# Expert routing in a fused attention and mixture kernel: positions, dummy products, and address tables per expert

## Chip, core and metric

The kernel runs on one core of a Trainium2 chip. The metric is device microseconds of one execution; a kernel's time is the median of its runs. An engine is named as the profile names it: PE is TensorE, DVE is VectorE, ACT is ScalarE, POOL is GpSimd, SP issues DMAs.

## What is computed

Attention in which each query keeps its 32 largest scores, then a soft mixture of experts (every token sends a weighted share to 32 slots), then a mixture in which each token goes to its two best experts of eight:

```python
def _moe2_ref(x, w_gate, w_noise, noise, w1, w2):      # x: 2304 x 512, w1: 8 x 512 x 1024, w2: 8 x 1024 x 512
    logits = x @ w_gate
    noisy_logits = logits + np.log1p(np.exp(x @ w_noise)) * noise
    top2 = np.argpartition(-noisy_logits, 2, axis=1)[:, :2]
    top2_l = np.take_along_axis(noisy_logits, top2, axis=1)
    top2_w = softmax(top2_l)                            # over the two
    for e in range(8):
        for k in range(2):
            mask = top2[:, k] == e
            h = np.maximum(x[mask] @ w1[e], 0.0)
            out[mask] += top2_w[mask, k, None] * (h @ w2[e])
    return out
```

x is itself a product of a 2304 x 32 matrix (the combine weights of the soft mixture, `cn`) with a 32 x 512 matrix of slot outputs (`so`). The kernel never forms x: it multiplies the slot outputs into the weights of each expert first ("expert e's weights" below are 32 x 1024), and routes rows of 32 numbers.

## The kernel before

The order of work is written out by hand: every engine executes its instructions in the order in which the program issues them, and semaphores make one engine wait for another. All products of float32 accuracy after the routing are made of three products of a high and a low half (`hh`, `hl`, `wh`, `wl`); the low half is a "correction" that VectorE subtracts.

The middle of the run has these stages, in `moe` and `gated`.

- *First mixture* (lines 825 to 906): eight experts' weights stream through; products per expert, the last expert's in two halves. Its end waits for the last weights.
- *Slot outputs and logits* (lines 907 to 1009): `cn` is transposed into `ct` (L912, L913), the slot outputs `sos` are folded (L823) into `soT`; the gate weights (L981) and `ct` (L989) give the logits of all tokens. Then expert 0's weights are multiplied (`weigh01`, L952, four quarters of eight products), while ScalarE and VectorE make the noisy logits `ng` and each token's eight largest (`m8`, L1009).
- *Routing of expert 0* (lines 1020 to 1170): one-hot `oh` (L1023), mask `mb` (L1026). TensorE first subtracts the high half of expert 0's weights (L1029, the correction), then counts, for each token, the tokens before it with the same expert (L1032 and 17 products of L1035): the position. `slot1` (L1042) holds expert 0's positions. `compact(t)` compares the positions of 128 tokens with the slot numbers (VectorE, L1148; four of 18 on ScalarE) and a product with the result (L1152) moves the tokens' rows to their slots. Expert 1's weights are multiplied between them.
- *Ramp* (`gated`, from line 1297): expert by expert, 64 chunks `n` = 8 e + c, with five products `acc` of three halves each per chunk. Chunk n issues `split(n + 2)` (halves of the second weights), `first(n + 2)` (L1254, then hh on ACT L1259 and hl on DVE L1260) and `second(n)` (L1278 to L1280). `first(n + 2)` needs the one buffer `hp`, which `hl` of the chunk before frees. After chunk 7 of an expert `store` scales the five accumulators (ACT and DVE in turn, L1288, L1290) and scatters them from GpSimd's queue (L1291); the next expert's `second` overwrites them.
- *Address tables* (`addresses`, `spread`, `rows_of_slots`): each token's slot number of 8 x 640 is split into a low part (slot modulo 128) and a column; one-hot tables of both, for 36 groups of 128 choices, are made by GpSimd, ScalarE and VectorE in chunk 0, and 36 products (L1125) in chunk 2 give the row number for every slot of all experts. Then GpSimd gathers rows by indirect DMA (`rows(e)`, L1223): expert 1 in chunk 2, expert 0 in chunk 4 (only its gates and token numbers are needed), expert 2 in chunk 6; `slots` and `turn` (L1242) bring them into place.

`order`, `slot` and `MORE` fix when the DMA queue of SP issues each expert's weights and into which buffer.

Of the kernel before, what the change touches and what calls it, by code (L numbers as in the profile page):

```python
# [8 lines left out]
F32 = mybir.dt.float32  # L9
F32R = mybir.dt.float32r  # L10
BF = mybir.dt.bfloat16
# [22 lines left out]
ED = 1  # L34
ONACT = (2, 6, 10, 14)
# [7 lines left out]
def moe_after_topk_attention(ctx: ExitStack, tc: tile.TileContext, q, k, v, phi, w1, w2, wg, wn, noise, u1, u2, qk, vt, qr, out):  # L43
# [3 lines left out]
    def pool(name, bufs=1, stack=ctx, **kw):  # L47
# [59 lines left out]
             + [(2, 0), (2, 1), (3, 0), (2, 2), (3, 1), (2, 3), (2, 4), (2, 5), (3, 2), (2, 6), (2, 7)]  # L107
# [3 lines left out]
    slot = [*range(11), 0, 1, 2, 3, 4] + [6, 0, 1, 2, 5, 6, 0, 2, 6, 1, 5] + [0, 2, 1, 5, 6]  # L111
# [64 lines left out]
    FW = (18, 19)  # L176

# [609 lines left out]
    def moe(st, xp, xs, fast):  # L787
# [26 lines left out]
        def warm(n):  # L814

            p = bank("acc0")
            for _ in range(n):
                T.matmul(p, onesb, onesb.unsqueeze(1).to_broadcast([128, 4, 128]), start=True, stop=True)
# [66 lines left out]

        sx, so = bank("acc2"), [bank(f"acc{n}") for n in range(2)]
        sos = ww[:, F + 2048:F + 2560]
        for e in range(E):
# [19 lines left out]
        ct = tb.tile([128, 5, 128], F32, name="ct")  # L908
        cf = cn.rearrange("p t s -> p (t s)")
        pc = [bank(x) for x in ("acc3", "acc2")]  # L910
        for g in range(4):
            T.transpose(pc[0][:, g * 128:g * 128 + 128], cf[:, g * 128:g * 128 + 128], identf)  # L912
        T.transpose(pc[1][:64, :128], cf[:, 512:576], identf)  # L913
        p = fold_t(sos, 4, fold)
        A.copy(ct[:, 0:4], pc[0].rearrange("p (a b) -> p a b", a=4))
        A.copy(ct[:64, 4], pc[1][:64, :128])
# [108 lines left out]
        mb = small("mb", BF)  # L1025
        V.tensor_tensor(mb, oh[:, 0], oh[:, 1], op=OP.add)  # L1026
        V.tensor_tensor(gw[:, 1], m8[:, :, 1], m8[:, :, 0], op=OP.subtract)
        for r, (x, h, _) in enumerate(quarters(0, P0)):
# [134 lines left out]
        for e in range(2):  # L1163
            used(2, e)
# [371 lines left out]
```

## Time and profile before

| | us |
|---|---|
| median of 3 runs | 753.01 (751.64 to 753.68) |
| profiled execution, its own time | 754.7 |
| its span, first to last instruction | 752.8 |

| engine | busy us | share of the span |
|---|---|---|
| PE matmul | 726.1 | 96% |
| PE weight load | 596.4 | 79% |
| DVE | 556.1 | 74% |
| POOL | 501.1 | 67% |
| ACT | 488.9 | 65% |

The shares are means over stages with different limits; matmuls are pipelined and overlap, so a busy PE isn't PE at its peak. The mean granted clock of TensorE over the span is 0.984 of full speed.

### The profile page before, as it was taken

The numbers are of one execution on the slowest core, as the hardware profiler recorded it, in microseconds if no ns is written. First come the engines' busy times: TensorE is split into PE (matmuls) and PEld (weight loads), VectorE is DVE, ScalarE is ACT, GpSimd is POOL, SyncE is SP. The second block draws the span as 40 slices with busy tenths as digits, with TensorE's granted clock in tenths as the row PEclk, the third lists the DMA queues.
The fourth block names the chain that finished last, engine by engine and source line by source line (L and its number), as shares of the span: only waits on it lengthen the run. The fifth ranks groups of instructions, "written<-read, shape, count | busy, mean of one in ns | idle before, by whom it ended". The sixth has DMA issues, their size and how long they took to land.

```text
span 752.8 us, 17317 instructions
## 1 busy us (share of the span) xinstructions
PE 726.1 (96%) x5670; PEld 596.4 (79%) x5670; DVE 556.1 (74%) x2632; ACT 488.9 (65%) x1025; POOL 501.1 (67%) x633
## 2 busy tenths in 40 slices
PE   9999999999999999999999998889999999999994
PEld 4789999898998889998898434567876888888883
DVE  7999999998999999999984404956554556555550
ACT  5999999999999999999995204742222222322320
POOL 4999999998999989999774030455551527344034
PEclk9999999999999999999999996999999999999998
DMA  6247687867786445544558799769774985344055
GB/s 222 51 114 224 184 227 211 224 193 185 205 223 187 108 119 112 130 112 110 155 217 284 267 392 344 263 255 346 177 144 139 320 279 72 61 65 61 1 64 72
DMA packets 62455, 133.99 MB, mean 178 GB/s; under 512 B 13330, under 2 KB 14354, under 8 KB 62354
## 3 DMA queue, kind: packets, MB, share of 16 engines
q1 hardware_dynamic: 55314, 122.59, 54.1%
q0 software_dynamic: 7040, 10.18, 9.8%
q8 instruction: 47, 0.77, 0.4%
q14 instruction: 54, 0.44, 0.2%
HBM read 85.02 MB, written 17.97 MB: 137 GB/s over the span
## 4 chain that ended last, share of the span: by engine, by line
PE 52%; DVE 26%; POOL 10%; issue 6%; DMA 3%; ACT 1%; SPq 0%; POOLq 0%; DVEq 0%; ACTq 0%
DVE c L506 10%; PE acc L1280 9%; PE acc L1279 9%; PE acc L1278 9%; DVE TH L537 5%; PE av L570 5%; POOL u L529 5%; DVE c L513 4%; PE S L468 3%; POOL s L544 2%; PE hp L1254 2%; PE st L549 2%; DVE mx L509 2%; DMA wx<-in_moe_w_dram 2%; PE acc L832 2%
## 5 line engine op out<-in xcount | busy, mean ns | idle before, releaser
L506 DVE MAX8 c<-s 128x8 f32<-128x82 f32 (+1 forms) x1008 | 221.4, 229 | 3.7 <-ACT s L486 3.0
L529 POOL TENSOR_TENSOR u<-g,s 128x576 f32<-128x576 bf16 x144 | 186.7, 1297 | 9.2 <-ACT g L523 9.2
L570 PEld LDWEIGHTS av<-vb,et 128*128 128x128 f32 (+1 forms) x1600 | 165.4, 180 | 11.2 <-issue 8.3
L570 PE MATMUL av<-vb,et 128*128 128x65 f32 (+1 forms) x1600 | 173.1, 263 | 0.8 <-ACT et L556 0.8
L1291 POOL DMA_INDIRECT out_dram<-y,ii x40 | 64.8, 1621 | 121.6 <-issue 60.2
L1259 ACT ACTIVATE hh<-hp 128x640 fp32r<-128x640 f32 x62 | 43.8, 707 | 136.9 <-PE hp L1254 136.9
L1278 PE MATMUL acc<-wh,hh 128*128 128x512 f32 x320 | 127.1, 397 | 0.6 <-DVE hl L1260 0.6
L1280 PE MATMUL acc<-wh,hl 128*128 128x512 f32 x320 | 126.9, 397 | 0.7 <-DVE hl L1260 0.7
L1279 PE MATMUL acc<-wl,hh 128*128 128x512 f32 x320 | 126.3, 395 | 0.0
L544 POOL TENSOR_SCALAR s<-s,mx 128x576 f32<-128x576 f32 x144 | 108.4, 753 | 21.2 <-ACT a L543 13.9
L537 DVE MAX8 TH<-u 128x8 f32<-128x584 f32 x144 | 109.1, 758 | 14.5 <-POOL u L530 13.6
L1260 DVE SCALAR_TENSOR_TENSOR hl<-hp,hh 128x640 fp32r<-128x640 f32 x62 | 51.1, 824 | 91.2 <-ACT hh L1259 91.1
L543 ACT ACTIVATE a<-s,TH 128x576 bf16<-128x576 f32 x144 | 117.4, 815 | 0.1
L549 PE MATMUL st<-identf,s 128*128 128x128 f32 x576 | 115.2, 281 | 1.4 <-POOL s L544 0.8
L523 ACT ACTIVATE g<-s,T 128x576 bf16<-128x576 f32 x144 | 116.4, 808 | 0.0
L550 PE MATMUL st<-steep,a 128*128 128x128 bf16 x576 | 105.5, 219 | 0.0
L468 PE MATMUL S<-ks,qs 128*128 128x288 f32 x560 | 105.1, 313 | 0.0
L488 ACT ACTIVATE s<-S 128x576 f32<-128x576 f32 x141 | 96.8, 687 | 4.5 <-PE S L477 2.6
L561 ACT ACTIVATE et<-st 128x512 f32<-128x512 f32 x144 | 90.4, 628 | 3.2 <-PE st L550 2.5
L549 PEld LDWEIGHTS st<-identf,s 128*128 128x128 f32 x576 | 83.6, 145 | 9.9 <-POOL s L544 3.3
L468 PEld LDWEIGHTS S<-ks,qs 128*128 128x128 f32 x560 | 78.6, 189 | 1.8
L1278 PEld LDWEIGHTS acc<-wh,hh 128*128 128x128 f32 x320 | 60.6, 190 | 14.9 <-issue 2.7
(339 smaller groups left out, 1151.0 us busy)
## 6 DMA issues: line engine op xcount, KB each, us to landing
wa<-in_moe_w_dram SPq DMA_DIRECT2D x8, 2048.0 KB, 13.9
wa<-in_moe_w_dram SPq DMA_DIRECT2D x28, 512.0 KB, 6.9
wb<-in_moe_w_dram SPq DMA_DIRECT2D x5, 2048.0 KB, 9.8
ks<-hl SPq DMA_DIRECT2D x56, 160.0 KB, 2.8
ks<-raw SPq DMA_DIRECT2D x56, 160.0 KB, 3.1
raw<-in_qk_dram SPq DMA_DIRECT2D x14, 608.0 KB, 4.5
wy<-in_moe_w_dram SPq DMA_DIRECT2D x4, 2048.0 KB, 9.3
wb<-in_moe_w_dram SPq DMA_DIRECT2D x16, 512.0 KB, 8.1
```

The source lines that it names most:

```text
L468: T.matmul(ph[hf][:, :288], QS[h][:, q0:q0 + 128], KS[h][:, l, ks], start=(n == 0), stop=(n == len(mm) - 1))
L506: V.max(C[i][:, c * 8:c * 8 + 8], SS[i][:, cut[c]:cut[c + 1]])
L523: A.activation(g, SS[i], AF.Sign, bias=last8(T24, i, 1), scale=-OVER, accum_out=SM[:, i:i + 1])
L529: G.tensor_tensor(u[:, 0:S], G1[i], SS[i], op=OP.mult)
L537: V.max(last8(TH, i), UU[i])
L543: A.activation(AP[i // 2][:, S * (i % 2):S * (i % 2) + S], SS[i], AF.Relu, bias=last8(TH, i, 1), scale=-1.0)
L544: G.tensor_scalar(SS[i], SS[i], -1.0, MX[i][:, 0:1], op0=OP.mult, op1=OP.add)
L549: T.matmul(o, SP[i // 2][:, ks], identf, start=True, stop=True, is_transpose=True)
L570: T.matmul(av[h][o:o + m, tt * 65:tt * 65 + 65], x, VB[j % 2][:, h, c if c < 4 else 4 + i % 2], start=(c == 0), stop=(c == 4), tile_positi ...
L1278: T.matmul(ACC[j], HH[n][:, r], WH[n], start=(c == 0), stop=False)
L1279: T.matmul(ACC[j], HH[n][:, r], WL[n], start=False, stop=False)
L1280: T.matmul(ACC[j], HL[n][:, r], WH[n], start=False, stop=(c == 7))
```

## The change

- The transposes of `cn` (`turn_c`) are issued ahead of the last expert of the first mixture. The fold of the slot outputs is written out, with two dummy products (`warm`, 512 columns of ones) between its halves and two behind it.
- The first quarter of expert 0's products stands ahead of the logits' product, the other three behind it, followed by nine dummy products.
- The mask comes straight from `ng` and `m8`, ahead of the one-hot; the positions come ahead of the correction of expert 0's weights.
- `slot1` holds the positions of experts 0 and 1 (`ED` 2). ScalarE makes three of the 18 compares (7, 11, 15). Expert 1's first two quarters of products come ahead of all compaction.
- The routed rows are written to DRAM from GpSimd's queue.
- The address tables are made in three parts. Expert 1 and expert 0 have their own (18 groups of 128 tokens each): columns by GpSimd (`slots_of`) beside the compaction, compares by VectorE, one per group (`hots_of`), 18 products each in chunks 2 and 4. Experts 2 to 7 share one: addresses in chunk 5, columns in chunk 6 (VectorE), compares in chunks 6 to 9 (VectorE and ScalarE), 36 products in chunk 9.
- The weights of expert 3 are loaded ahead of the second weights of expert 1. The flags for the rare cases are made in chunk 21, with a new test of ties (`keep_tie`). Expert 2's slots and turns come one chunk later.

```diff
-ED = 1
-ONACT = (2, 6, 10, 14)
+ED = 2
+ONACT = (7, 11, 15)
...
-             + [(2, 0), (2, 1), (3, 0), (2, 2), (3, 1), (2, 3), (2, 4), (2, 5), (3, 2), (2, 6), (2, 7)]
+             + [(2, 0), (2, 1), (3, 0), (2, 2), (2, 3), (3, 1), (2, 4), (2, 5), (3, 2), (2, 6), (2, 7)]
...
+    LATER = 21
...
+        def turn_c():
+            cf = cn.rearrange("p t s -> p (t s)")
+            x = halves()
+            for g in range(4):
+                T.transpose(x[:, 0, g * 128:g * 128 + 128], cf[:, g * 128:g * 128 + 128], identf)
+            T.transpose(x[:64, 1, :128], cf[:, 512:576], identf)
+            A.copy(ct[:, 0:4], x[:, 0].rearrange("p (a b) -> p a b", a=4))
+            A.copy(ct[:64, 4], x[:64, 1, :128])
...
             if e == E - 2:
                 A.copy(sos, sx)
+                turn_c()
...
+        p = bank()
+        for c in range(4):
+            if c == 2 and fast:
+                warm(2, "acc3")
+            T.matmul(p[:, c * 32:c * 32 + 32], sos[:, c * 128:c * 128 + 128], fold, start=True, stop=True)
+        p = p[:, :4 * NS].rearrange("p (c s) -> p c s", s=NS)
+        if fast:
+            warm(2, "acc3")
...
+        if fast:
+            P0, P1 = bank("acc1"), bank("tp")
+            weigh01(0, 0, P0)
         ggd = tb.tile([128, 4, 16], F32, name="ggd")
...
         if fast:
-            P0, P1 = bank("acc1"), bank("tp")
-            for c in range(4):
+            for c in range(1, 4):
                 weigh01(0, c, P0)
+            warm(9, "acc2")
...
+        mb = gp.tile([128, TT, 8], BF, name="mb")
+        V.tensor_tensor(mb, ng, m8[:, :, 1:2].to_broadcast([128, TT, 8]), op=OP.is_ge)
         V.tensor_tensor(oh, ng.unsqueeze(1).to_broadcast([128, 2, TT, 8]),
...
-            nc.sync.dma_start(XD[0:2 * NTOK].rearrange("(p r) f -> p (r f)", p=128), RW.rearrange("p c t f -> p (c t f)"))
+            G.dma_start(XD[0:2 * NTOK].rearrange("(p r) f -> p (r f)", p=128), RW.rearrange("p c t f -> p (c t f)"))
...
+        def hot(o, x, on_act=False):
+            if not on_act:
+                for i in range(x.shape[-1]):
+                    V.tensor_scalar(o[:, i], ntb, x[:, i:i + 1], None, op0=OP.is_equal)
+                return
...
+        def slots_of(e):
...
+            for j in range(JT + 1):
+                G.tensor_scalar(ge[:, :, j], slot1[:, :, e], 128.0 * j + 1, 0.0, op0=OP.is_ge, op1=OP.add)
+            G.tensor_tensor(eq, ge[:, :, 0:JT], ge[:, :, 1:], op=OP.subtract)
+            G.tensor_scalar(w, oh[:, 1, :, e], float(TT), 0.0, op0=OP.mult, op1=OP.add)
+            G.tensor_tensor(w, w, ctn[:, 0:TT], op=OP.add)
+            G.tensor_tensor(x[:, :, 0], eq, w.unsqueeze(2).to_broadcast([128, TT, JT]), op=OP.mult)
+            G.tensor_scalar(x[:, :, 1], eq, pn, 0.0, op0=OP.mult, op1=OP.add)
...
             def columns():
...
+                V.tensor_tensor(eq, nt[:, 2 * JT:E * JT].unsqueeze(1).to_broadcast([128, 2 * TT, m]),
+                                pc[:, 1].unsqueeze(2).to_broadcast([128, 2 * TT, m]), op=OP.is_equal)
+                V.tensor_tensor(x[:, :, 0], eq, ctn.unsqueeze(2).to_broadcast([128, 2 * TT, m]), op=OP.mult)
+                V.tensor_scalar(x[:, :, 1], eq, pn, None, op0=OP.mult)
...
-        more(20)
-        for n, c in zip((3, 3, 3, 3), range(4)):
+        used(2, 0)
+        more(21)
+        for e in (1, 0):
+            slots_of(e)
+        for n, c in zip((0, 0, 2, 3), range(4)):
             some(n)
             weigh01(1, c, P1)
-        for e in range(2):
-            used(2, e)
-        some(2)
+        used(2, 1)
+        some(7)
         gates()
+        low_of()
         some(TT)
...
             if n == 0:
-                begin()
-                for k in range(3):
-                    far(k)
-                    near(k)
-                columns()
-                partitions()
-                for k in range(3, 5):
-                    same(k)
+                halve1(1, P1)
+                hots_of(t2, 1, (0,))
+            if n == 1:
+                hots_of(t2, 1, (1, 2))
...
             if n == 3:
-                first_weights2(ps.tile([128, 512], F32, name="tp"))
+                first_weights2(tp())
+                hots_of(t2, 0, range(3))
             if n == 4:
+                p1 = tp()
+                join_of(0, p1)
+                rows_in(t2, p1, 0, 1)
+                rows(0)
+                ids_of(0)
                 slots(1)
-                rows(0)
             if n == 5:
                 turn(1, 0, 4)
+                addresses()
             if n == 6:
-                ids_of(0)
+                columns, hots, join = spread(t2)
+                columns()
+                hots(0, True)
+            if n == 7:
+                hots(2, False)
+            if n == 8:
+                hots(1, True)
+                for i in (3, 4):
+                    hots(i, False)
+            if n == 9:
+                hots(5, False)
+                p1 = tp()
+                join(p1)
+                rows_in(t2, p1, 2, E - 2)
                 rows(2)
-            if n == 9:
                 ids_of(2)
+            if n == LATER:
+                later(t2)
...
-                if c == 3 and e:
+                if c == (4 if e == 1 else 3) and e:
                     slots(e + 1)
-                if c == 4 and e:
+                if c == (5 if e == 1 else 4) and e:
                     turn(e + 1, 0, 4)
```

`hots`, `join`, `hots_of`, `join_of` and `store` stand in program order within a chunk as the list shows; `store` is issued last in chunk 7.

## Rows read from the trace of the kernel before

**Rows 1.** Stretches: PE, PEld, DVE, ACT, POOL busy (count), clock, DMA share, GB/s.
```profile
456.30:470.00 13.70, 11.44 (x87) 5.99 (x90) 7.07 (x35) 8.01 (x18) 0.00 (x0) 0.50 0.96 317
...
488.20:493.20 5.00, 1.63 (x37) 1.46 (x36) 4.97 (x5) 3.80 (x6) 2.96 (x2) 1.00 0.93 338
...
493.90:497.20 3.30, 3.30 (x9) 2.61 (x8) 1.99 (x6) 1.13 (x2) 1.93 (x2) 0.50 1.02 416
...
500.00:735.00 235.00, 234.06 (x1123) 186.44 (x1122) 129.03 (x221) 64.02 (x100) 97.00 (x80) 1.00 0.59 141
```

**Rows 2.** Chain of waits, 430 to 512 us: start, us, what.
```profile
433.82 17.46 DMA wx<-in_moe_w_dram
...
457.51 3.61 PE acc L952 x32
...
501.16 3.57 PE tp L1210 x32
```

**Rows 3.** Instructions in order of time, compaction: start, us, what, [idle before].
```profile
465.35 2.80 DVE L1148 TENSOR_SCALAR wx<-nt,slot 128x128 fp32r<-128x128 f32 x7
...
473.56 1.95 PE L1152 MATMUL acc<-wx,xw 128*64 128x320 f32 x12
```

**Rows 4.** Instructions in order of time, SP's queue: expert 0's weights issued.
```profile
439.12 2.54 SPq L134 DMA_DIRECT2D wb<-in_moe_w_dram  x1
```

**Rows 5.** DMA issues at that time: KB each, median us to landing.
```profile
wb<-in_moe_w_dram SPq DMA_DIRECT2D x1, 2048.0 KB, 17.1
```

**Rows 6.** Instructions in order of time, logits to positions.
```profile
455.61 1.90 PE L989 MATMUL acc<-ggd,ct 128*128 128x64 f32 x10 [0.45 <-DVE ggd L984]
...
457.55 0.29 ACT L1001 ACTIVATE na<-acc 128x144 f32<-128x144 f32 x1 [3.35 <-PE acc L989]
...
459.27 1.32 DVE L1009 MAX8 nz<-T 128x8 f32<-128x8 f32 x18
...
461.11 0.31 DVE L1026 TENSOR_TENSOR mb<-oh 128x144 bf16<-128x144 f32 x1
...
463.69 0.30 PE L1032 MATMUL acc<-mb,before 128*128 128x144 bf16 x1
```

**Rows 7.** Instructions in order of time, ramp: VectorE beside GpSimd.
```profile
478.57 6.51 POOL L1095 TENSOR_TENSOR y<-nt,pc 128x1024 bf16<-128x1024 f32 x3 [36.26 <-ACT hh L1259]
...
478.98 2.04 DVE L1270 TENSOR_TENSOR wl<-wa,wh 128x512 fp32r<-128x512 f32 x1
```

**Rows 8.** VectorE's groups by shape, 430 to 600 us: busy us, mean ns, idle before.
```profile
L1270 DVE TENSOR_TENSOR wl<-wb,wh 128x512 fp32r<-128x512 f32 x16 | 11.2, 698 | 0.5
...
L1109 DVE TENSOR_TENSOR eq<-nt,pc 128x800 bf16<-128x800 f32 x1 | 1.0, 984 | 0.0
...
L1148 DVE TENSOR_SCALAR wx<-nt,slot 128x128 fp32r<-128x128 f32 x1 | 0.3, 286 | 0.1
```

**Rows 9.** Instructions in order of time, GpSimd, 430 to 480 us.
```profile
437.15 0.66 POOL L850 COPY RW<-LT 128x576 f32<-128x576 f32 x1
437.75 0.21 POOL L851 COPY RW<-ids 128x18 f32<-128x18 f32 x1
```

**Rows 10.** Instructions in order of time, ramp: chunks, turns, corrections.
```profile
477.24 0.51 PE L1278 MATMUL acc<-wh,hh 128*128 128x512 f32 x1
...
506.03 1.39 DVE L1216 TENSOR_TENSOR gl<-tp,gh 64x512 fp32r<-64x512 f32 x2 [5.32 <-ACT gh L1213]
...
513.53 0.33 PE L1242 MATMUL tp<-identf,cx 128*128 128x128 f32 x1 [0.68 <-ACT cts L1244]
...
515.08 0.46 PE L1254 MATMUL hp<-cts,gs 128*128 128x320 f32 x2
...
516.31 0.82 DVE L1260 SCALAR_TENSOR_TENSOR hl<-hp,hh 128x640 fp32r<-128x640 f32 x1 [3.31 <-ACT hh L1259]
...
526.82 0.46 PE L1254 MATMUL hp<-cts,gs 128*128 128x320 f32 x2
...
530.56 0.46 PE L1254 MATMUL hp<-cts,gs 128*128 128x320 f32 x2
```

More of the change, by code (lines that the diff above doesn't have):

```diff
@@ L1022, in moe @@
         oh = gp.tile([128, 2, TT, 8], F32, name="oh")
+        mb = gp.tile([128, TT, 8], BF, name="mb")
+        V.tensor_tensor(mb, ng, m8[:, :, 1:2].to_broadcast([128, TT, 8]), op=OP.is_ge)
         V.tensor_tensor(oh, ng.unsqueeze(1).to_broadcast([128, 2, TT, 8]),
                         m8[:, :, 0:2].rearrange("p t c -> p c t").unsqueeze(3).to_broadcast([128, 2, TT, 8]), op=OP.is_equal)
[L1025 to L1028, printed above, removed]
-            T.matmul(x, minus, h.bitcast(F32), start=False, stop=True, tile_position=(0, 32 * r), skip_group_check=True)
+        below = gp.tile([128, TT], F32, name="below")
+        V.tensor_tensor(below, m8[:, :, 1], m8[:, :, 0], op=OP.subtract)
         pos = bank("acc3")
@@ L1038, in moe @@
         T.matmul(tot[:, :144], onesb, mbf, start=True, stop=True)
+        for r, (x, h, _) in enumerate(quarters(0, P0)):
+            T.matmul(x, minus, h.bitcast(F32), start=False, stop=True, tile_position=(0, 32 * r), skip_group_check=True)
         tots = SM
@@ new lines, in tiles @@
+        def tiles(t2, n):
+            return [t2.tile([128, min(6, n - i), 128], BF, name="lt", bufs=6) for i in range(0, n, 6)]
+        low = gp.tile([128, TT, ED], F32, name="low")
+        def slots_of(e):
+            w = gp.tile([128, TT], F32, name=f"w{e}")
+            ge = gp.tile([128, TT, JT + 1], F32, name=f"ge{e}")
+            eq = gp.tile([128, TT, JT], F32, name=f"eq{e}")
+            x = first_e[e] = gp.tile([128, TT, 2, JT], BF, name=f"x{e}")
+            for j in range(JT + 1):
[5 more added lines that the diff above has]
+            G.tensor_scalar(x[:, :, 1], eq, pn, 0.0, op0=OP.mult, op1=OP.add)
@@ new lines, in low_of, with hots_of, join_of @@
+        def low_of():
+            z = gp.tile([128, 2, TT, ED], I32, name="z")
+            V.tensor_scalar(z[:, 0], slot1, 127.0, None, op0=OP.add)
+            V.tensor_scalar(z[:, 1], z[:, 0], 127, None, op0=OP.bitwise_and)
+            V.tensor_scalar(low, z[:, 1], 1.0, None, op0=OP.add)
+        def hots_of(t2, e, some):
+            if e not in hots_e:
+                hots_e[e] = tiles(t2, TT)
+            for i in some:
+                hot(hots_e[e][i], low[:, 6 * i:6 * i + 6, e])
+        def join_of(e, p):
+            x, lt = first_e[e], hots_e[e]
+            for i in range(TT):
+                T.matmul(p[:, 0:2 * JT], lt[i // 6][:, i % 6], x[:, i].rearrange("p a j -> p (a j)"), start=(i == 0),
+                         stop=(i == TT - 1))
@@ L1299, in gated, with tp @@
         gather()
-        addresses()
         done()
         tl, t2 = pool("tl", 4, st), pool("t2", 2, st)
-        pairs, far, near, same, columns, partitions = spread(t2)
+        hots_of, join_of, rows_in = routes
+        def tp():
+            return ps.tile([128, 512], F32, name="tp")
         first(0)
@@ L1308, in gated @@
             e, c = divmod(n, 8)
-            if (e, c) == (1, 0):
-                later(t2)
             m = n + 2
@@ L1317, in gated @@
                 second(n, range(2))
+                if m < 8 * E and n != 6:
+                    first(m)
                 if n == 2:
-                    rows_of_slots(ps.tile([128, 512], F32, name="tp"), pairs)
-                if m < 8 * E:
+                    p1 = tp()
+                    second(n, [2])
+                    join_of(1, p1)
+                second(n, range(3 if n == 2 else 2, JT))
+                if n == 6:
                     first(m)
-                second(n, range(2, JT))
             elif n == 8 * E - 4:
```

97 lines of the change are left out of this document (41 added, 56 removed).

## Prediction

> **What bounds the kernel now.** I read the busy time by stretches first, then the chain of waits of the middle of the run, then the order of work on each engine there. From 500 to 735 us TensorE is busy 234.06 of 235.00 us at full clock [rows 1]: nothing that only moves work about can help there, and what is won must be won before 500. The chain of waits shows why nothing is won before 451.3 either: it runs through the DMA that brings the last expert weights of the first mixture [rows 2], and the change reorders no load ahead of that one. So the change lives in 49 us, from 451.3 to 500. Two losses stand in it. The granted clock is 0.50 (1.2 GHz) from 456.3 to 470.0, and again 0.50 from 493.9 to 497.2, after TensorE had been busy only 1.63 us of the 5.00 before, while VectorE was busy 4.97 of them [rows 1]. The first loss is the routing (logits, top two, positions, compaction of expert 0's rows), a serial chain that hops between engines. The second is the ramp, in which VectorE builds the address tables of all experts while TensorE waits.
>
> **The change, part by part.** The sum is made in the clock of the profiled execution (754.7 us, its span 752.8; the median of the runs is 753.0, so 1.7 less) and the difference is then taken from 753.0. C is the end of the last compaction product, 473.56 + 1.95 = 475.5 before [rows 3].
>
> *Transposes and fold.* Five transposes leave the path (they go into the wait for the last weights), two dummy products come into it between the halves of the fold. A dense 512-wide product costs 234.06 / 1123 = 0.21 us at full clock [rows 1], so 0.4 comes back, and the transposes hold up the last products of the first mixture by a little. I call it even, 0.4 either way.
>
> *Expert 0's products ahead of the logits.* The first quarter of them now stands in TensorE's queue before the logits' product (L989). Its weights were issued at 439.12 [rows 4] and took 17.1 us to land [rows 5]: 456.2. TensorE executes in order, so the logits wait for that DMA: the eight products take 0.45 to 0.9 of it (8/32 of 3.61 at the low clock [rows 2], half of that at the full one), and L989 starts at 456.8 where it started at 455.61 [rows 6]. That is 1.2 us lost. L989 took 1.90, of which 0.7 was before the clock fell and 1.2 after [rows 1, 6]; with the clock held it is 0.7 + 0.6 = 1.3. The logits are then ready at 458.1 instead of 457.5: 0.6 later.
>
> *Mask before the one-hot.* The mask now needs only the eight maxima. They ended at 459.27 + 1.32 = 460.59 and the mask started at 461.11 [rows 6]: 0.5 saved. Mask ready: 461.42 + 0.6 - 0.5 = 461.5.
>
> *Positions ahead of the correction.* Before, the positions' product stood behind the correction of expert 0's weights, which waits for ScalarE, and started at 463.69 [rows 6]. Now 24 products of expert 0 and nine dummies stand ahead. The 32 products took 3.61 at the low clock [rows 2]; 24 of them at twice the clock are 1.4, nine dummies 1.9: 458.1 + 3.3 = 461.4, just before the mask. Positions start at 461.5, 2.2 earlier. From there to the first compare went 465.35 - 463.69 = 1.66 [rows 3, 6], of which about 1.3 is products at the low clock: 1.0 now. First compare: 462.5, 2.85 earlier.
>
> *Compaction.* VectorE does 15 compares instead of 14. Seven of 3,456 elements took 2.80 [rows 3], 0.81 ns each; the 15 have 8,320: 6.7 us. Between them stand seven narrow operations (gates, slots modulo 128), each between 0.07 (a narrow maximum, 1.32 / 18) and 0.31 (the mask) [rows 6]; 0.19 taken: 1.3. With 0.4 for the last products C is 462.5 + 8.4 = 470.9. TensorE needs less: 35 products at 1.95 / 12 [rows 3], 5.7, and expert 1's at full clock, 1.8. Gain 4.6.
>
> *Columns on GpSimd.* 22 small GpSimd operations now run beside those compares. The trace of before has GpSimd idle there, so I bound it from the ramp: while GpSimd ran three wide products in 6.51 us, a correction on VectorE took 2.04 us [rows 7], where its mean in the later stage is 0.70 [rows 8]. It lost 1.3 us to operations of 2.2. A narrow GpSimd copy takes 0.21, a 32 times wider one 0.66 [rows 9], so most of 0.21 is a fixed cost. Bounds: nothing, or 15 compares each held for a whole 0.21, 3.2 us. I take 22 times 0.05, 1.0, nearer the narrow end, since the elements are few. The Trainium skill (SBUF — State Buffer, SBUF: two separate sides) says that the pair of ports that VectorE shares with GpSimd is an exclusive lock for a whole instruction; the stretched correction agrees. By that rule taken whole the 1.0 would be 3.2, and the sum worse by 2.2. C is 471.9, 3.6 us earlier than before.
>
> *The ramp, from C to the middle of chunk 10.* Before: 530.56 - 475.5 = 55.0 [rows 10]. After: the first expert product 1.7 behind C as before (477.24 [rows 10]), 0.4 until the first correction (its six address operations have moved away); ten chunks and 0.37 of one at 530.56 - 526.82 = 3.74: 38.8; the product of experts 2 and 3's weights, 3.6 [rows 2]; 72 address products instead of 36 at 1.63 / 37 = 0.044 [rows 1]: 3.2; the turn of expert 1's rows, 0.6 and its wait of 0.7 [rows 10]. Sum 49.0. Then VectorE's order makes two new waits.
> First, chunk 4: expert 0's 18 compares stand behind the correction of experts 2 and 3's weights, which ended 507.4 - 504.7 = 2.7 behind that product [rows 2, 10]. A 128-wide compare took 0.286 alone [rows 8] and less back to back; 0.19 taken, between 0.07 and 0.286. 2.7 + 18 x 0.19 + 0.25 for the last six products = 6.4; TensorE is there after 3.74 + 0.7: it waits 1.9 (0 to 3.6).
> Second, chunk 8: its first products overwrite accumulators that VectorE must have scaled out. In its queue, from the end of expert 1's first product: 1.6 to the end of that correction (515.5 to 517.1 [rows 10]); three wide operations for the columns of experts 2 to 7, 1,080 elements each, at 0.984 for 800 [rows 8] two of 1.3 and one, from one input, of 0.6; the next weights' halves 1.1 and correction 0.8; six compares 1.1; the output 0.7. That is 8.5, and TensorE is there after 3.74 + 0.35 + 0.7 = 4.8: it waits 3.7 (3.0 at the cheap compare, 4.3 at the dear one). With 0.35 in chunk 7 (its buffer comes free only with the late correction of chunk 8's) the ramp is 49.0 + 6.0 = 55.0: even with before, since it gives back what the wait for the tables and the slow 3.3 us cost.
>
> *Later.* The two turns of expert 2's rows now stand back to back on one buffer; the first such pair waited 0.68 [rows 10]: +0.7. At no cost: the write of the routed rows on GpSimd's queue (about 10 us before the first gather; cover gone, it would be the landing itself), the load of expert 1's second weights behind expert 3's first ones (both are issued before chunk 1 and the former are needed from chunk 6 on; cover gone, VectorE would wait for them there), the flags at chunk 21, where VectorE has nothing else extra.
>
> Sum: -3.6 + 0.0 + 0.7 = -2.9, and 753.0 - 2.9 = 750.1.
>
> **The rivals.** *The dummies turn against the path.* TensorE idles from about 455.3 to 456.2 for expert 0's weights, more than the 0.45 that it idled there before [rows 6], and before the clock fell at 456.3. If it falls again, eight products, L989, 24 products and nine dummies at 0.43 run at 1.2 GHz: 456.2 + 0.9 + 2.3 + 2.7 + 3.8 = 465.9, positions 2.2 later than before, C at 465.9 + 1.7 + 8.4 + 1.0 = 477.0, 1.5 later; with the turn's 0.7, 755.2, and 756.8 if the ramp's wait brings the low clock too. It decides when positions start after 463.7, before's time. Against it: the four dummies around the fold are denser work than anything that stood there. If the clock comes back midway, about 753.
> *GpSimd holds VectorE for whole operations* (the upper bound above, 15 x 0.21 = 3.2 in place of 1.0): 752.3. The stretched correction speaks for it, the few elements against. The lock that the Trainium skill's page names would act so.
> *The ramp's clock falls.* Some 3.5 us of idle time near chunk 8, as the 3.4 of 5.0 us before 493.9 [rows 1]; half of 3.3 us: +1.6, 751.7.
> *VectorE is not late in the ramp.* If compares cost 0.07 and the columns come cheap, the waits of 1.9 and 3.7 stay out: 744.5. Against it: the column operations are the same form as the row of 0.984.
> *The dummies do nothing to the clock in the routing* is the first rival; the change then does not do what it says.
>
> **How the numbers follow.** Forecast 0.40 (its own range 748.5 to 751.5, by half the bounds of its unknown costs), dummies against the path 0.18, clock back midway 0.08, GpSimd's hold 0.10, the ramp's clock 0.10, no waits in the ramp 0.14. A measurement tells 0.3% (2.3 us) from no change. Faster than 750.7 are the last case and 0.33 of the forecast: 0.47. Slower than 755.3 is the first rival, mostly with the ramp's low clock behind it: 0.18. The rest is 0.35. The range 745.5 to 755.5 takes in the bounds of GpSimd's hold (749.1 to 752.3) and of the compare (747.5 to 752.4), and leaves out the ramp without any wait and the worst of the first rival.
>
> **What would show it.** The logits' first product waiting for a DMA of the second mixture's weights, at about 456; the granted clock at 1.00 between 456 and 470; positions starting near 461.5; the last compaction product near 472; a wait of TensorE on a VectorE compare in the address product of expert 0; its longest wait of the ramp at chunk 8 on VectorE's output scaling. Wrong would be: no DMA wait (then another 1.2 us), a low clock past 460, or a chunk 8 without a wait.

## The result and the profile after

The changed kernel takes 761.35 us (median of 4 runs, 759.87 to 764.06) where the kernel before takes 752.55 (751.64 to 753.68): 1.012 times as long, with a 95% interval of 1.0085 to 1.0156. The forecast was 750.1, with a range of 745.5 to 755.5, so it was wrong, and by its sign. The span of the profiled execution is 762.2 us, 9.4 longer than before.

The first thing to look for is where the forecast and the trace part. Up to the end of the compaction they don't. The lines that answer to [rows 3, 6], instructions in order of time after the change (start, us, what, [idle before <- what ended it]):

```profile
456.42 0.64 PE L964 MATMUL acc<-wb,soT 128*32 128x256 f32 x8 [0.91 <-DMA wb<-in_moe_w_dram]
456.99 1.44 PE L1004 MATMUL acc<-ggd,ct 128*128 128x64 f32 x10
458.36 1.50 PE L964 MATMUL acc<-wb,soT 128*32 128x256 f32 x24
459.79 2.12 PE L819 MATMUL acc<-onesb 128*128 128x512 bf16 x9
461.54 0.31 DVE L1039 TENSOR_TENSOR mb<-T,nz 128x144 bf16<-128x144 f32 x1
461.91 0.24 PE L1047 MATMUL acc<-mb,before 128*128 128x144 bf16 x1
463.07 4.13 DVE L1197 TENSOR_SCALAR wx<-nt,slot 128x128 fp32r<-128x128 f32 x10
...
469.12 2.57 PE L1201 MATMUL acc<-wx,xw 128*64 128x320 f32 x12 [0.22 <-DVE wx L1197]
```

The first quarter of expert 0's products waits for its weights and starts at 456.42, the logits follow at 456.99, the nine dummies end as the mask is ready, the positions start at 461.91 instead of 463.69 [rows 6], and the last compaction product ends at 469.12 + 2.57 = 471.69 instead of 475.5 [rows 3]. The clock held through the routing and was lost at another place, as the stretches show (PE, PEld, DVE, ACT, POOL busy, then the granted clock, the DMA share and GB/s), to be read beside [rows 1]:

```profile
456.00:470.00 14.00, 13.36 (x136) 7.54 (x136) 10.28 (x46) 8.71 (x19) 6.62 (x17) 1.00 0.95 309
474.00:483.00 9.00, 0.15 (x1) 0.00 (x1) 0.71 (x2) 1.52 (x4) 0.00 (x0) 0.69 1.00 368
483.00:488.00 5.00, 4.97 (x13) 4.09 (x14) 3.10 (x7) 2.27 (x6) 0.00 (x0) 0.54 0.90 349
```

From 474 to 483 hardly an engine does anything: TensorE is busy 0.15 of 9.00 us, VectorE 0.71, ScalarE 1.52, GpSimd 0. Only the DMA share is full. Then TensorE works, at a mean granted clock of 0.54, so at the lower of its two levels (1.2 GHz) for most of that stretch. What ended the hole stands in the instructions of that stretch, and once more in the chain of waits (the last line):

```profile
467.87 0.27 DVE L1069 COPY RW<-gw 128x36 f32<-128x36 f32 x1
...
472.72 0.82 POOL L1070 DMA_DIRECT2D xd<-RW  x1
482.29 0.89 DVE L1317 SCALAR_TENSOR_TENSOR hl<-acc,hh 128x320 fp32r<-128x320 f32 x2 [9.46 <-DMA xd<-RW]
483.03 0.76 PE L1337 MATMUL acc<-wh,hl 128*128 128x512 f32 x1 [8.88 <-DVE hl L1317]
...
472.72 9.47 DMA xd<-RW
```

The first correction `hl` of the ramp waits 9.46 us for the DMA that writes the routed rows (RW) to DRAM (XD), and TensorE waits 8.88 us for that correction. Neither tensor is an operand of the correction. What they share is memory. This is where the program's layout puts three pools, in bytes of each partition (it is printed by the program, not by the profile):

```text
pool (what lies in it)                    before             after
tb (RW, xw, ct; closed before the ramp)   178816 to 196576   179104 to 196576
tl (hl)                                   165632 to 175872   169440 to 179680
t2 (tables, gathered rows, outputs)       175872 to 203016   179680 to 216712
```

The new tiles, most of them for the tables of experts 0 and 1, made the pool in front of `hl` larger by 3,808 bytes. The pool of `hl`, which ended 2,944 bytes below RW's pool, now reaches 576 bytes into it. RW itself starts at 187840, far above. The buffer that the first correction writes, 169440 to 172000, lies below all of RW's pool; only the last of the four buffers of `hl` reaches into it. Yet in the built program, right ahead of the first correction, VectorE has a wait for the semaphore that this write raises. So the wait goes by pools, not by tiles. The theory on this: the first tile of a pool that takes over memory of a closed one waits for everything that still reads or writes that one, the read by the DMA included. The rivals: GpSimd's queue makes the write slow or holds VectorE up; or the ramp is late for VectorE's order anyway, and the hole only comes first.

### The profile page after: what moved, and what is told of

Its sections match the earlier page's. It is cut to its first block, busy times and chain, and to the rows that moved or that the text cites. A ratio compares the mean times of both kernels' runs of the same rounds, so it can differ in the third digit from the quotient of the medians.

```text
span 762.2 us, 17512 instructions
## 1 busy us (share of the span) xinstructions
PE 729.9 (96%) x5719; PEld 599.0 (79%) x5719; DVE 563.2 (74%) x2705; ACT 485.2 (64%) x1029; POOL 499.4 (66%) x652
## 4 chain that ended last, share of the span: by engine, by line
PE 51%; DVE 26%; POOL 10%; issue 6%; DMA 4%; ACT 1%; SPq 0%; POOLq 0%; DVEq 0%
DVE c L507 10%; PE acc L1335 9%; PE acc L1337 9%; PE acc L1336 9%; DVE TH L538 5%; PE av L571 5%; POOL u L530 5%; DVE c L514 4%; PE S L469 3%; PE hp L1311 2%; DVE mx L510 2%; PE st L550 2%; DMA wb<-in_moe_w_dram 2%; POOL s L545 2%; PE acc L833 2%
## 5 line engine op out<-in xcount | busy, mean ns | idle before, releaser
L1337 PEld LDWEIGHTS acc<-wh,hl 128*128 128x128 f32 x320 | 61.2, 191 | 22.7 <-issue 9.3
```

What stands on the lines that cost most here:

```text
L1337: T.matmul(ACC[j], HL[n][:, r], WH[n], start=False, stop=(c == 7))
```

## The experiments

Ratios are to the kernel before, run on the same chip; intervals are 95%.

**RW in a pool of its own.**

```diff
+        rwp = pool("rwp", 1, st)
         for i in range(4):
             wpool[f"wy{i}"] = pool(f"wy{i}", 1, ta_st)
...
-                    RW = tb.tile([128, 2, TT, ROW], F32, name="RW")
+                    RW = rwp.tile([128, 2, TT, ROW], F32, name="RW")
```

> The changed kernel with one difference: the tile RW (the routed rows) lies in a pool of its own that stays open, so no later tile takes over its memory; instructions, queues and order are the same. Theory (the first correction hl waits 9.46 us because its pool takes over memory of the pool that holds RW, whose write to DRAM is still being read): the wait of hl on the DMA is gone, TensorE's hole from 474.15 to 483.03 is gone, and so is the low clock that followed it (4.7 us at half speed, 2.3 us): 761.4 - 8.9 - 2.3 = 750.1, between 749 and 752. Rival (the write from GpSimd's queue costs by itself, its transfer or its instructions holding up VectorE): at least 757. Rival (the ramp is late for its VectorE waits in chunks 4 and 8, and these grow as the hole goes): 753 to 757.

754.46 us (753.42 to 758.52), ratio 1.0021 (1.0001 to 1.0040). VectorE waits 0.57 us ahead of the first correction, for ScalarE's `hh` and no longer for a DMA; the hole is gone. But the time lies 2.5 us above the expected upper end. SP's queue shows one reason: the group of weight loads `wy` of the first mixture took 6.8 us longer to issue. Its pools (`wy`) stand behind the new one, hence 5,184 bytes higher, over memory that the stage before them still used. The first correction in rw_apart, then the group of loads there and in the changed kernel, then what SP waited for in rw_apart (us in total, times, longest):

```profile
476.59 0.97 DVE L1318 SCALAR_TENSOR_TENSOR hl<-acc,hh 128x320 fp32r<-128x320 f32 x2 [0.57 <-ACT hh L1317]
```

```profile
391.86 28.24 SPq L134 DMA_DIRECT2D wy<-in_moe_w_dram  x4
```

```profile
390.90 21.49 SPq L134 DMA_DIRECT2D wy<-in_moe_w_dram  x4
```

```profile
SPq L134 <- PE st L351: 11.2, 1, 11.2
```

The cure moved the ailment: another pool came to lie over memory in use. That is enough for the 2.5 us: the last compaction products end at 472.30 + 2.57 = 474.87 there, 3.2 later than in the changed kernel.

```profile
472.30 2.57 PE L1202 MATMUL acc<-wx,xw 128*64 128x320 f32 x12 [0.21 <-DVE wx L1198]
```

So the next versions leave everything ahead of the ramp where it was.

**Only `hl` clear of RW's pool.** Two scratch tiles of `slots_of` are shared between the two experts, which takes 832 bytes away in front of `hl`; its pool ends at 178848.

```diff
-            ge = gp.tile([128, TT, JT + 1], F32, name=f"ge{e}")
-            eq = gp.tile([128, TT, JT], F32, name=f"eq{e}")
+            ge = gp.tile([128, TT, JT + 1], F32, name="ge")
+            eq = gp.tile([128, TT, JT], F32, name="eq")
```

> The changed kernel with two scratch tiles of slots_of shared between experts 1 and 0: 832 bytes less per partition in front of the pool of hl, which now ends at byte 178848, below RW's pool (from 179104); in the changed kernel it ended at 179680 and reached 576 bytes into it. Theory (it is this overlap that makes hl wait): hl no longer waits for the DMA. The next pool still lies over RW's, so the wait moves to its first tile, the first compares of expert 1's table in chunk 0, which VectorE reaches near 478.5; the write lands near 482.2, so VectorE waits 2 to 4 us there, and TensorE loses somewhat less: 751.5 to 754.5. Rival (the wait goes by tiles, and hl's tiles are not what lies over RW): hl waits as before, 761.4.

754.60 us (750.28 to 757.28), ratio 1.0009 (0.9988 to 1.0029), just above what was expected. The first correction has no DMA wait any more. The wait is where the theory puts it, at the first tile of the next pool. That tile lies at 178848 to 180384, so it doesn't touch RW's own bytes either (instructions in order of time):

```profile
473.86 0.97 DVE L1317 SCALAR_TENSOR_TENSOR hl<-acc,hh 128x320 fp32r<-128x320 f32 x2 [0.57 <-ACT hh L1316]
...
482.36 1.07 DVE L1108 TENSOR_SCALAR lt<-ntb,low 128x128 bf16<-128x128 bf16 x6 [2.44 <-DMA xd<-RW]
...
484.94 0.56 PE L1311 MATMUL hp<-cts,gs 128*128 128x320 f32 x2 [1.88 <-DVE hl L1317]
```

832 bytes are worth 6.8 us by the medians (761.35 to 754.60) and 1.1% by the ratios (1.0120 to 1.0009), with not one instruction more or less.

**The write ahead of expert 0's columns.**

```diff
-        for e in (1, 0):
-            slots_of(e)
+        slots_of(1)
...
         gates()
+        slots_of(0)
```

> The changed kernel with the 11 GpSimd instructions of slots_of(0) behind the gates and the write of RW instead of ahead of them. In the changed kernel the gates were ready at 468.13 and GpSimd issued the write at 472.72. Theory: issued near 468.3; if the transfer still takes 9.5 us it lands near 477.7, the hole is 4.4 us shorter: 755.5 to 757.5. If the transfer is what is slow, because weights share the DMA engines, it lands little earlier: 759 to 761. If it is quick without POOL's small operations behind it, under 755.

758.12 us (754.91 to 759.48), ratio 1.0060 (1.0040 to 1.0080), somewhat above the 755.5 to 757.5 expected. GpSimd issued the write at 467.68 instead of 472.72, and `hl` waited half as long:

```profile
467.68 0.82 POOL L1070 DMA_DIRECT2D xd<-RW  x1 [0.38 <-DVE z L1136]
```

```profile
476.83 0.89 DVE L1317 SCALAR_TENSOR_TENSOR hl<-acc,hh 128x320 fp32r<-128x320 f32 x2 [4.79 <-DMA xd<-RW]
```

From issue to the correction went 9.15 us, against 9.57 in the changed kernel: issued five us apart, the transfer takes some nine us in both. So the hole is 4.6 us of GpSimd's queue (gates ready at 468.14, issue at 472.72) and 9.5 of transfer, less what VectorE has to do in that time.

**The write back on SP's queue.**

```diff
-            G.dma_start(XD[0:2 * NTOK].rearrange(...), RW.rearrange(...))
+            nc.sync.dma_start(XD[0:2 * NTOK].rearrange(...), RW.rearrange(...))
```

> The changed kernel with the write of RW back on SP's queue, at the same place in the program; the memory is as in the changed kernel. SP then issues it behind the loads of experts 2 and 3's and expert 1's second weights, which it had done issuing at 478.0 in the changed kernel, so at 478 rather than 472.7. Theory (the hole lasts until this write has landed, whichever queue it is on): it lands behind them, near 485, and hl waits until then, 12 us instead of 9.5: 763 to 766. Rival (GpSimd's queue is what made the write slow): below 758.

763.68 us (760.29 to 765.64), ratio 1.0129 (1.0105 to 1.0154): as long as with GpSimd's queue, or longer. The expectation had SP issue it at 478; it was issued at 468.23, behind two loads of 2 MB (466.25 and 467.64) and ahead of the others, and yet landed no sooner:

```profile
468.23 0.41 SPq L1070 DMA_DIRECT2D xd<-RW  x1
```

```profile
483.04 0.89 DVE L1317 SCALAR_TENSOR_TENSOR hl<-acc,hh 128x320 fp32r<-128x320 f32 x2 [10.18 <-DMA xd<-RW]
```

GpSimd's queue is not what the hole needs: on SP's the transfer took 14.7 us from issue to landing.

**The kernel before, with only the write moved to GpSimd's queue.**

```diff
-            nc.sync.dma_start(XD[0:2 * NTOK].rearrange(...), RW.rearrange(...))
+            G.dma_start(XD[0:2 * NTOK].rearrange(...), RW.rearrange(...))
```

> The kernel before with one difference: RW is written from GpSimd's queue, not SP's. There the pool of hl ends at byte 175872, below RW's pool (from 178816), so hl cannot wait; the first tiles that lie over RW's pool are the one-hot tables that GpSimd starts at 478.57. Theory: GpSimd is idle, issues at 472.9, the write lands 9.5 us later at 482.4, the tables start 3.8 us later and the address product with them: 755 to 757. Rival (on record in the prediction: the write from GpSimd's queue costs nothing): 752.5 to 753.

754.87 us against 753.55, ratio 1.0023 (1.0010 to 1.0035): a small loss, just below what was expected and above the prediction's nothing. With `hl` clear, the first tile over RW's pool is GpSimd's own table. GpSimd starts it 7.72 us after the issue, 5.5 us behind the last compaction product of that run (474.07) where it was 478.57 - 475.5 = 3.1 before [rows 3, 7]:

```profile
471.86 0.83 POOL L1053 DMA_DIRECT2D xd<-RW  x1 [29.28 <-DVE wx L1148]
479.58 6.19 POOL L1095 TENSOR_TENSOR y<-nt,pc 128x1024 bf16<-128x1024 f32 x3 [6.88 <-ACT hh L1259]
```

The row names ACT's `hh` as what ended the wait; the table's operands had been there since 476.83. In the built program the table waits for this write beside five other semaphores, so the write's landing is the likelier reason; the row doesn't show it.

**All pools clear** of the write while it runs. On top of the shared scratch tiles, the pool of tables, gathered rows and outputs is put over the compaction's own buffers (which lie above 196576; it now takes 198784 to 229320), and the two column tiles of chunk 6 in a small pool of their own. That one still lies over RW's pool, but is first written in chunk 6, long after the landing.

```diff
-        tl, t2 = pool("tl", 4, st), pool("t2", 2, st)
+        tl, t2, t4 = pool("tl", 4, st), pool("t2", 2, st, side="right"), pool("t4", 1, st)
...
-            x = t2.tile([128, 2 * TT, 2, m], BF, name="x6", bufs=1)
-            eq = t2.tile([128, 2 * TT, m], BF, name="eq6", bufs=1)
+            x = t4.tile([128, 2 * TT, 2, m], BF, name="x6")
+            eq = t4.tile([128, 2 * TT, m], BF, name="eq6")
```

> The changed kernel with the pools laid so that nothing of the ramp's first chunks lies over the pool of RW: two scratch tiles shared (hl's pool ends below it), the pool of the tables, gathered rows and outputs put where the compaction's compares were, and the two column tiles of chunk 6 in a pool of their own. Instructions, queues and order are the same. Theory (the pools' memory is the whole of the miss's largest part): neither hl nor the first compares wait for the write of RW; against the version in which only hl was clear (754.6) the compare's wait of 2.44 us on VectorE and TensorE's 1.88 us behind it go: 752 to 753. Rival (the ramp's other waits grow by what is won): 754.6 again.

749.44 us (747.02 to 752.66), ratio 0.9958 (0.9938 to 0.9979): better than expected, and next to the forecast of 750.1. Instructions, queues and order are those of the changed kernel, so 761.35 - 749.44 = 11.9 us, more than the whole of the miss, is where the pools lie. The last rival, a ramp that is late for VectorE's order anyway, is out with it. The ramp's first stretch, against 0.15 busy of 9.00 in the changed kernel:

```profile
475.00:480.00 5.00, 5.00 (x25) 4.25 (x24) 4.42 (x10) 4.09 (x10) 0.00 (x0) 1.00 0.97 329
```

**Expert 0's compares earlier**, on this layout.

```diff
-                first_weights2(tp())
                 hots_of(t2, 0, range(3))
+                first_weights2(tp())
```

> The same layout, and expert 0's 18 compares put ahead of the products of experts 2 and 3's weights in chunk 3, where VectorE stood idle for 6.3 us (from 491.8 to 498.2). Theory (chunk 4's wait is VectorE's order): the 18 address products no longer wait (about 2.2 us of 2.95), and the low clock that followed (0.62 to 0.69 from 500 to 510, 1.5 to 3 us) goes with it: 2 to 4 us below the same layout alone. Rival (the products wait for something else, or the wait moves on to chunk 8): less than 1 us below.

747.21 us (746.09 to 748.01), ratio 0.9935 (0.9915 to 0.9955). The 18 address products of chunk 4, first without and then with the edit:

```profile
497.09 2.21 PE L1148 MATMUL tp<-x,lt 128*128 128x10 bf16 x18
```

```profile
496.00 0.61 PE L1148 MATMUL tp<-x,lt 128*128 128x10 bf16 x18
```

1.6 us were wait for VectorE. The median gained 2.2, at the lower edge of the 2 to 4 expected, with an interval that meets that of the layout alone. The two executions that these rows are from took 747.37 and 747.52, so the row's 1.6 us doesn't show in their time: that the edit gains is not shown.

**Experts 2 to 7's columns earlier**, on this layout.

```diff
             if n == 5:
                 turn(1, 0, 4)
                 addresses()
+                columns, hots, join = spread(t2, t4)
+                columns()
             if n == 6:
-                columns, hots, join = spread(t2, t4)
-                columns()
```

> The same layout, and the three column operations of experts 2 to 7 (3.0 us of VectorE) put behind the addresses of chunk 5, ahead of chunk 6, in which VectorE stood idle for 4 to 5 us. Theory (chunk 8's wait is VectorE's queue): the wait of 2.45 us of chunk 8's product on the scaled output goes, with the smaller ones before it (0.3 each): 2.5 to 3.5 us below the same layout alone. Rival (the output's scaling is late for its own reasons, ScalarE's scaling and compares): under 1 us below.

745.85 us (744.40 to 746.25), ratio 0.9915 (0.9889 to 0.9941), 3.6 us below the layout alone. Chunk 8's wait, first without and then with the edit:

```profile
516.40 0.50 PE L1335 MATMUL acc<-wh,hh 128*128 128x512 f32 x1 [2.45 <-DVE y L1345]
```

```profile
515.08 0.50 PE L1335 MATMUL acc<-wh,hh 128*128 128x512 f32 x1 [0.95 <-DVE y L1345]
```

The wait lost 1.5 us, not the whole 2.45, and the two executions that the rows are from, 747.37 and 745.89, lie as far apart; the rest of the 3.6 is not in these two rows. In the runs of the layout alone the granted clock of the whole span went with the time: those at 0.996 took 747.0 to 747.8, those at 0.990 or 0.991 took 749.2 to 752.7. All four of this version have 0.996 or 0.997. A shorter wait that loses the clock less often would give the rest; it was not isolated.

**Both.**

> Both of these edits on the same layout. Theory: they add up, 4.5 to 7.5 us below the layout alone, 745 to 748, and faster than the kernel before by 0.7 to 1.1 per cent: what the prediction gave for a ramp without VectorE's waits was 744.5. Rival (the low clock has causes of its own): 749 to 751.

745.60 us (743.48 to 748.10), ratio 0.9907 (0.9879 to 0.9936): no better than the columns alone by what can be told, and 3.8 us below the layout alone where 4.5 to 7.5 were expected. The two gains don't add up.

**Without the 13 dummy products**, on the layout with all pools clear.

```diff
-            if c == 2 and fast:
-                warm(2, "acc3")
...
-        if fast:
-            warm(2, "acc3")
...
-            warm(9, "acc2")
```

> The changed kernel with the pools laid clear of RW (749.4), without its 13 dummy products in fold and routing. Theory of the prediction (the dummies keep TensorE at full clock there): the clock falls to 0.50 after the logits' inputs as in the kernel before, the expert's products and the logits' take 1.5 to 3 us more in the chain, the last compaction product ends 2 to 3.5 us later: 751.5 to 753. Rival (the denser work around the wait holds the clock without them): positions start as the mask is ready and the time is 749 to 749.7.

750.94 us (748.11 to 752.42), ratio 0.9971 (0.9958 to 0.9984): 1.5 us more by the medians, 1.0 by the ratios, less than the 751.5 to 753 expected and with intervals that overlap, so the time alone shows no loss. In the rows the clock falls where the prediction's first rival had it, the logits' product takes 2.53 us instead of 1.44, and the positions then wait for the mask, which is late (stretch, then instructions):

```profile
456.00:458.00 2.00, 2.00 (x15) 1.38 (x7) 0.00 (x0) 0.00 (x0) 0.00 (x0) 0.50 1.04 408
```

```profile
456.63 2.53 PE L1000 MATMUL acc<-ggd,ct 128*128 128x64 f32 x10
...
462.63 0.22 PE L1042 MATMUL acc<-mb,before 128*128 128x144 bf16 x1 [0.75 <-DVE mb L1034]
```

From the landing of expert 0's weights to the positions it took 462.63 - 455.62 = 7.0 us, with the dummies 461.91 - 456.42 = 5.5 in the changed kernel. So the dummies bought 1.5 us of the routing there; the edit removes all 13, so which of them hold the clock isn't told apart. They don't always hold it: of the ten traces with all 13 the clock is 1.00 from 456 to 470 in nine; in that of experts 2 to 7's columns earlier it fell to 0.50 although all are there, and there too the positions started 462.48 - 455.51 = 7.0 us behind the landing:

```profile
458.00:460.00 2.00, 2.00 (x21) 0.75 (x14) 1.83 (x15) 0.55 (x3) 0.00 (x0) 0.50 1.02 387
```

```profile
455.51 0.64 PE L964 MATMUL acc<-wb,soT 128*32 128x256 f32 x8 [0.92 <-DMA wb<-in_moe_w_dram]
...
462.48 0.23 PE L1047 MATMUL acc<-mb,before 128*128 128x144 bf16 x1
```

**Expert 0's first quarter behind the logits again**, same layout.

```diff
             P0, P1 = bank("acc1"), bank("tp")
-            weigh01(0, 0, P0)
...
-            for c in range(1, 4):
+            for c in range(4):
                 weigh01(0, c, P0)
```

> The changed kernel with the pools laid clear of RW (749.4), with the first quarter of expert 0's products behind the logits' product again. Theory: TensorE no longer waits 0.91 us for their weights ahead of the logits, which are 1.1 to 1.3 us earlier; but 32 products and nine dummies (4.1 us) then stand between logits and positions, and the positions gain only 0.4 to 0.9 us: 748.5 to 749.1. Rival (the quarter held the clock through the wait): the clock falls and it is 750 to 752.

747.37 us (745.73 to 754.37), ratio 0.9946 (0.9922 to 0.9971). The logits no longer wait for the weights (0.45 us for their own operand instead of 0.91 for the DMA), and the clock stayed at 1.00. The median is 2.1 us below that of the layout alone (0.9 by the ratios) and 1.1 below the expected range, but the intervals overlap widely and the runs lie 8.6 us apart: a gain is not shown.

**All that helped, with seven dummies instead of nine.**

> The edits that helped, together: the pools clear of RW, expert 0's compares ahead of the products of experts 2 and 3's weights, the columns behind the addresses of chunk 5, all of expert 0's products behind the logits, and seven dummies in the routing instead of nine (with nine they ended 0.3 us behind the mask). Theory: with both ramp edits 745.6 was measured; the logits' order is worth 0.4 to 0.9 more and the two dummies 0.3: 744 to 745. Rival (the earlier positions only move the ramp's start, and the weights of the next experts come no earlier): 745.6 again.

745.90 us (744.18 to 746.88), ratio 0.9904 (0.9889 to 0.9919): faster than the kernel before by 0.96%, and no faster than both ramp edits without the rest, as the rival had it. The last compaction product ended at 470.44, 36.25 us behind the issue of the last weights of the first mixture where the layout alone took 37.61, and then a new wait stood at the head of the ramp:

```profile
472.06 0.82 PE L1310 MATMUL acc<-cts,gs 128*128 128x320 f32 x4 [1.62 <-DMA gs<-gl]
```

```profile
472.00:476.00 4.00, 3.85 (x13) 3.01 (x14) 2.93 (x6) 2.44 (x6) 0.30 (x1) 0.67 1.03 412
```

Expert 0's weights are turned by a DMA through SP's queue (`gs<-gl`), and that is now late. It was late in the version before too, by a wait of 1.09 us; these two have all of expert 0's products behind the logits. In the rest the product waited for ScalarE's `cts`. The clock falls there too. By these rows a routing that is faster still would gain nothing in the ramp before that DMA is earlier too; no run tries it.

## Why the prediction was wrong, and where it was right

**The step that failed** is the one sentence under *Later*: "At no cost: the write of the routed rows on GpSimd's queue (about 10 us before the first gather; cover gone, it would be the landing itself)". It looked for readers of what the write makes, the gathers, and there it was right: the first gather came at 497.17. It didn't look at who takes over what the write *reads*. It also left out that GpSimd had 22 instructions ahead of the write, which set when it was issued, and that new tiles move the pools behind them, which set what had to wait for it. The landing that the sentence names in brackets is what came: 9.47 us after the issue, on the path, and TensorE's low clock behind it. No rival had this place. Of the two edits behind it the memory alone is enough: with the write on SP's queue as before and the memory moved, 763.7; with the queue changed and the memory as before, 754.9 against 753.6; with the queue changed and the pools clear, 749.4. Why the transfer itself takes nine us or more stays open.

**The rest of the sum stood.** Its terms, measured in the changed kernel and, where the hole disturbs them, on the layout with all pools clear (its profiled execution took 747.37):

| step | predicted | measured |
|---|---|---|
| logits' product starts | 456.8 | 456.99 |
| mask ready | 461.5 | 461.54 + 0.31 = 461.85 |
| positions start | 461.5 | 461.91 |
| last compaction product ends | 471.9 | 471.69 |
| GpSimd's hold on VectorE there | 1.0 (0 to 3.2) | 0.3 |
| a 128-wide compare, back to back | 0.19 | 3.02 / 18 = 0.17 |
| wait of chunk 4 on expert 0's compares | 1.9 (0 to 3.6) | 2.21 - 0.61 = 1.6, pools clear |
| wait of chunk 8 on the output | 3.7 (3.0 to 4.3) | 2.45 + 0.30 + 0.28 = 3.0, pools clear |
| from there to chunk 12's first product | 55.0 | 68.1; 525.81 - 472.07 = 53.7, pools clear |
| median | 750.1 | 761.35; 749.44, pools clear |

That the median with the pools clear comes within 0.7 us of the forecast is in part luck. Four of its ten executions, at a granted clock of 0.996, took 747.0 to 747.8, 2.3 to 3.1 below the forecast. The other six lost clock at some place, for which the sum has no term, and brought the median back up.

The 68.1 less the 53.7 are 14.3 us. 9.9 of them lie ahead of the first product for chunk 2 (the hole of 8.9, and the low clock behind it), 1.1 more from there to that of chunk 6 (low clock until near 488), and 3.3 from there to that of chunk 12, where the clock falls behind the waits of chunks 4 and 8 in the changed kernel and not in this execution of the other. The compares and address products of chunk 4 in the changed kernel, then the stretch behind them there, then with all pools clear:

```profile
507.13 3.02 DVE L1108 TENSOR_SCALAR lt<-ntb,low 128x128 bf16<-128x128 bf16 x18
507.77 2.61 PE L1148 MATMUL tp<-x,lt 128*128 128x10 bf16 x18
```

```profile
511.70:514.50 2.80, 2.80 (x8) 2.36 (x8) 2.53 (x8) 0.70 (x1) 1.79 (x2) 0.50 1.04 404
```

```profile
500.00:510.00 10.00, 9.08 (x43) 6.95 (x41) 6.72 (x20) 3.12 (x8) 5.14 (x5) 1.00 1.04 408
```

**Terms that were off, with the mechanism right.** *GpSimd beside the compares* was put at 1.0 us. The mean compare of 640 columns took 572 ns with GpSimd's 22 instructions beside it, and 550 before, without (VectorE's groups by shape, busy us, mean ns; after, then before):

```profile
L1197 DVE TENSOR_SCALAR wx<-nt,slot 128x640 fp32r<-128x640 f32 x11 | 5.6, 572 | 0.0
```

```profile
L1148 DVE TENSOR_SCALAR wx<-nt,slot 128x640 fp32r<-128x640 f32 x11 | 5.5, 550 | 1.8 <-PE acc L1152 1.2 <-ACT wx L1145 0.6
```

22 ns for each of 15 is 0.3 us. The rule that the prediction weighed, the exclusive lock that the Trainium skill (SBUF — State Buffer, SBUF: two separate sides) describes, would have made it 3.2 taken whole; the section ties the lock to a two-port mode or two SBUF inputs, which the prediction left out. Another section of that page (Who interferes with whom) leaves out a VectorE instruction with at most one SBUF input that isn't in a two-port mode; no row here says which mode these compares were in, only that VectorE wasn't held for whole operations. *GpSimd's own instructions* were the term to get right: 22 at 0.21 [rows 9] are 4.6 us, and they took from 463.07 to 472.72, 9.65, for 0.44 each. The groups of six compares show it, 0.46 and 0.37 each (GpSimd, in order of time):

```profile
463.07 2.74 POOL L1126 TENSOR_SCALAR ge<-slot 128x18 f32<-128x18 f32 x6 [20.36 <-DVE slot L1059]
...
468.02 2.22 POOL L1126 TENSOR_SCALAR ge<-slot 128x18 f32<-128x18 f32 x6
```

If one engine held the other there, GpSimd is the likelier one to have waited. The same addition took 0.73 us in the changed kernel, beside a subtraction on VectorE, and 0.23 in the run with the write ahead of expert 0's columns, where VectorE stood idle:

```profile
471.26 0.68 DVE L1327 TENSOR_TENSOR wl<-wa,wh 128x512 fp32r<-128x512 f32 x1
471.29 0.73 POOL L1129 TENSOR_TENSOR w<-w,ctn 128x18 f32<-128x18 f32 x1
```

```profile
472.10 0.23 POOL L1129 TENSOR_TENSOR w<-w,ctn 128x18 f32<-128x18 f32 x1
```

The prediction asked only what GpSimd's operations do to VectorE, not what VectorE does to them.

*Later* held 0.7 for the turns of expert 2. The stretch from chunk 12's first product to the end took 222.24 us before, 222.44 after and 219.8 with all pools clear; it varies by more than the term, which no run isolates, and why it is 2.4 shorter there is open.

**The rivals.** The dummies did not turn against the path: the clock was 1.00 from 456 to 470 in the changed kernel, and in the trace without them it is 0.50 from 456 to 458. The ramp's low clock, put at 1.6 us for chunk 8 alone, came in the changed kernel behind chunk 4 as well. GpSimd's whole-operation hold on VectorE is out. "VectorE is not late in the ramp", 744.5, is about what the kernel gives when its waits are taken away by order: 745.6 to 745.9.

## What to carry to other kernels

When an edit moves a DMA later or to another queue, look not only for the readers of what it writes but for who next takes over the memory that it reads; and when an edit adds tiles, print where every pool lies before and after, since some hundred bytes can hang the next stage on a transfer that it has nothing to do with. An engine's wait on a DMA whose tensors it doesn't touch is the mark of this in a profile. Work that stands ahead of a DMA issue on an in-order engine is priced by its count times its own duration beside its neighbours, not by a copy measured elsewhere.

## What the runs showed of the hardware

A write of 648 KB took 9.5 us from GpSimd's queue and 14.7 from SP's behind two weight loads, while the DMA share was near 1.00 with weight loads on the same engines. By the Trainium skill (DMA: Bandwidth & Descriptors, Anatomy of one DMA — SWDGE path) such a write alone is 2.0 us and its bytes at 436 GB/s, by estimate 3.5 us; no run here shows it alone, so how much of the rest the loads beside it add is open. The other thing: after a hole of 8.9 us TensorE's granted clock stood at a mean of 0.54 for the next five, so the hole cost more than its length.
